# First four heads loaded head by head on two queues, the first two chunks' order rewritten, constants set by VectorE, one share moved by two groups

## The chip, the cores and the metric

The kernel runs on one core of a Trainium2 chip. The core has a matrix engine (TensorE, written PE in the profile, with its weight loads as PEld), VectorE (DVE), ScalarE (ACT), GpSimd (POOL) and SyncE (SP), which here only issues DMAs. The five run side by side, each through its own instruction list in order, and wait for one another on semaphores. The metric is the device time of one execution in microseconds (us); lower is better. Three executions of the kernel before took 309.56, 308.94 and 307.16 us (median 308.94). A further execution, the one with the profile, took 308.46 us; its span from the first to the last instruction is 306.7 us, so 1.76 us lie around the span.

## The reference, cut to what matters

```python
# q, k, v: (4, 8, 768, 64) float32; proj: (64, 6); x has 4 x 768 rows of 512
q_bits = einsum('bhsd,dk->bhsk', q, proj) > 0        # 6 sign bits: the bucket; k likewise
mask   = q_bucket[:, :, :, None] == k_bucket[:, :, None, :]
scores = where(mask, scale * q @ k.T, -1e9)
attn   = softmax(scores)
x      = (attn @ v) as (batch, seq, heads * 64)
xn     = (x - mean) / sqrt(var + 1e-6) * g_ln
out    = x + relu(xn @ w_ch1) @ w_ch2                # 512 -> 2048 -> 512
```

Attention looks only at keys whose 6 hash bits equal those of the query. An MLP with a residual follows.

## The kernel before, in words

The work is 12 chunks: 4 batches x 3 chunks of 256 queries. A chunk has 12 units (`att_units`), four pairs of heads by three groups of key blocks. Unit u has four steps: S (scores: four matmuls into one `sc` tile, L452), X (one exp over 128x1024 on ScalarE, L462), V (eight matmuls of the exps with the values into `av`, L487; the first unit of a pair adds one matmul with the key epsk, L476, in batch 0), and, at the third unit of a pair, D (the division on VectorE, L505 to L514). Then the chunk's MLP runs (row statistics L533, centring L539, up products L596 with a relu each on DVE or ACT, down products L637 and the residual L642), spread as filler between the units of the next chunk.

The mask comes without a comparison: 6 bits as +-1/2 are put beside the 64 rows of each query and key in `slots`, so one matmul over 70 rows gives score and match together, and the exp makes a mismatch vanish.

Batch 0 has to be prepared before any attention can start, head by head. T(h) (L204, four transposes on PE) turns three pairs of key blocks and the first pair of query blocks of head h; E (L223 DVE, L221 ACT) copies the result out of PSUM, scaled; C casts its halves into `slots` (L248 DVE, L240 ACT, L242 POOL); H (L258, PE) hashes two heads at once; B (L268, DVE) compares with zero and writes the even bits; O (L240 ACT, L242 POOL) copies the odd bits. The same words with an L in front (LT, LE, LC, LH, LB, LO) do the remaining query blocks of two heads together, which chunks 1 and 2 need. vc casts values (L357, POOL), su and sd sum them (L381 PE, L388 DVE). T uses the PSUM bank `av1`, or `av0` where the word ends with an engine's letter, and the bank is free again when E and the C that read it are done. K is a run of idle matmuls that wake PE (L783), J puts the projection in place (L797, DVE), w starts weight and batch-1 loads from POOL's queue, n, ns, xt, xe, U, R are the first chunk's MLP, na, bl and op the preparation of batch 1 by DMA transposes.

For chunks 0 and 1 the order of all these steps is written out by hand in the string `opening`, played by `first_two`; each engine receives its own instructions in that order. From chunk 2 on, `interleave` places fillers between the units by cost, and two small tables add single steps: `singly` (squares on ACT) and `shares`. A share (L371, L372) is for batches 1 to 3: one matmul broadcasts the sum of values over partitions into the `av` bank that the running pair doesn't use, and DVE copies it to `vsum`; D adds it. The next pair's V takes that same bank.

Loads: `load_half` (L124 to L147) fetches q and k of four heads. For the first four heads of batch 0 it cuts the load at 0, 1, 2, 4: heads 0 and 1 singly (q from SP's queue, k from ACT's), heads 2 and 3 together, both q and k from SP's queue. Behind them on SP's queue come the values of heads 0 to 3, q and k of heads 4 and 5, q and k of heads 6 and 7, the second half of the values, and eight small loads of proj.

At the end every engine reads a flag (L939) and branches over a general path (L940) that isn't taken with these data. Two hints for that branch are given to DVE and ACT, before the last down products.

Of the kernel before, what the change touches and what calls it, by code (L numbers as in the profile page):

```python
# [18 lines left out]
LBIT = BIT * BIT  # L19

Q_SCALE = 2.0**-12
# [3 lines left out]
EPS_KEY = 2.0**-100  # L25
# [5 lines left out]
def kernel(  # L31
# [11 lines left out]
    nc = tc.nc  # L43
    P = 128

    B, H, S, D = q.shape
    n_bits = proj.shape[1]
# [9 lines left out]
    D1 = D + 1  # L57
    scale = 1.0 / math.sqrt(D)
# [5 lines left out]
    with tc.manual_schedule():  # L64
# [8 lines left out]
    identf = consts.tile([P, P], F32)  # L73
    make_identity(nc, identf)
    expb = consts.tile([P, 2], F32)
    nc.gpsimd.memset(expb[:, 0:1], -scale * n_bits * 0.25 / Q_SCALE)
    nc.gpsimd.memset(expb[:, 1:2], -scale * n_bits * LBIT)
    ident = consts.tile([P, P], BF16)
    make_identity(nc, ident)
    epsk = consts.tile([P, P], BF16)  # L80
    nc.gpsimd.memset(epsk, EPS_KEY)
    mhalf = consts.tile([P, TT], F32)
    nc.gpsimd.memset(mhalf, -0.5)
    sq = consts.tile([P, 2, 4 * B], F32)

    NG, DG = P // 32, D // 32
# [14 lines left out]
    vaug = [  # L101
        consts.tile([P, H, NC, D1], BF16, name=f"vaug{i}", tag=f"vaug{i}") for i in range(2)
    ]
# [2 lines left out]
    vsplit = consts.tile([P, H, D1], BF16)  # L106
    vsum = [consts.tile([P, H, D], F32, name=f"vsum{i}", tag=f"vsum{i}") for i in range(2)]
    for i in range(2):
        nc.gpsimd.memset(vaug[i][:, :, :, D:D1], 1.0)

    main = ExitStack()
    nat = main.enter_context(tc.tile_pool(name="nat", bufs=4))
# [16 lines left out]
    def load_half(b, half):  # L129

        h0 = half * H // 2
        t = {}
        for nm in "qk":
            t[nm] = nat.tile([P, H // 2, NC, D], F32, tag=f"{nm}nat", name=f"{nm}nat")

        cuts = [[0, 1, 2, 4] if half == 0 else [0, 2, 4], [0, 4], [0, 2, 4], [0, 2, 4]][b]
        for lo, hi in zip(cuts, cuts[1:]):
            for nm, src in (("q", q), ("k", k)):
                eng = nc.gpsimd if b == 1 else nc.scalar if nm == "k" and hi - lo == 1 else nc.sync
                eng.dma_start(  # L140
                    out=t[nm][:, lo:hi],
                    in_=src[b, h0 + lo : h0 + hi].rearrange("h (p c) d -> p h c d", p=P),
                )
        if b == 0 and half == 0:
            nc.scalar.activation(wake2[:, 0:1], wake2[:, 1:2], AF.Exp)
            t["v"] = load_values(b, half)
        return t  # L147

    def load_values(b, half):
        h0 = half * H // 2  # L150
        eng = nc.gpsimd if (b, half) == (1, 0) else nc.sync
        if (b, half) == (0, 1):

            t = work.tile([P, NH * CT // 2], F32, tag="h", bufs=1, name="vnat1")[
                :, 0 : H // 2 * NC * D
            ].rearrange("p (h c d) -> p h c d", h=H // 2, c=NC)
        else:
            t = nat.tile([P, H // 2, NC, D], F32, tag="vnat", bufs=1, name="vnat")
        eng.dma_start(
            out=t, in_=v[b, h0 : h0 + H // 2].rearrange("h (p c) d -> p h c d", p=P)  # L160
        )
        return t
# [3 lines left out]
    class Prep:  # L166
# [7 lines left out]
        def load(self, half):  # L174
            self.tiles.setdefault(half, {}).update(load_half(self.b, half))
# [573 lines left out]
    def chunk_tile():  # L749
# [4 lines left out]
    mlp = {0: mlp_steps(*chunks[0], xs[0])}  # L754

    opening = """
        K26 T0 E0d T1d C0.1g E1a J0 C0.0p C1.1g H0 T2 C1.0g E2a T3d B0 O0g B1 E3d C2.0a S0 C3.0p X0
        O1g LT0 C2.1g vc0 C3.1g S1 H1 X1 S2 LE0d T5d T4 B2 X2 O2g su0 E4a B3 w0 E5d S3 C4.0a sd0 T6d
        H2 E6d B4 C5.0a V0 C4.1a T7 O3g S4 V1 C5.1g E7d X3 O4a V2 X4 S5 vc1 H3 C7.1p B5 D2 V3d S6 X5
        C6.1g B6 X6 O5g V4 LT1d B7 S7 X7 C6.0g V5 C7.0g LE1d su1 O7g D5 S8 LH0 sd1 O6g X8 S9 LC1.0p  # L760
        V6d S10 X9 LB0 V7 LT2d LC0.0g w1 V8 LE2d LO0g LC0.1g D8 S11 LT3d LB1 X10 S12 LE3d X11 V9d w2
        X12 V10 V11 S13 V12 LC3.0g D11 S14 X13 n0 LO1g LC1.1g n1 LH1 ns1 S15 LC2.1g ns0 V13 X14 S16
        V14 LB2 xt0 LB3 X15 LC2.0g V15 xe0d LO2g S17 X16 S18 bl3 V16 bl0 LO3g U0 D14 X17 U1 V17 X18
        R0a S19 LC3.1g R1d V18 X19 bl2 U2 S20 R2d U3 w3 X20 S21 U4 D17 R3a X21 V19 S22 R4a na0 U5
        bl1 R5a X22 na1 S23 U6 V20 U7 V21 D20 R6d S24 R7d V22 X23 V23 X24 nr0 op0 D23
    """

    def first_two():
# [91 lines left out]
    singly = {  # L860
        2: "Q00", 3: "Q01", 4: "Q10", 5: "Q11", 6: "Q20", 7: "Q21", 8: "Q30", 9: "Q31",
    }
    shares = {2: {8: "E10"}, 3: {5: "E11"}, 5: {1: "E20", 10: "E21"}, 7: {1: "E30"}, 8: {1: "E31"}}
    parts_left = {}

    def prepare(op):
# [53 lines left out]
    with tc.manual_schedule():  # L920
        held["up"](NH // 2 - 1)
        norm[1]()
        held["relu"](NH // 2 - 1, nc.scalar)
        for _, f in tail:
            f()
        for n2 in range(NH // 2):
            parts["up"](n2, True)
            parts["relu"](n2, nc.scalar if n2 % 2 else nc.vector)
        for _, f in downs[: 4 * (TT - 1)]:
            f()  # L930
        tc.mark_branch_hint_location(
            "general", "LikelyTaken", [nc.vector.engine, nc.scalar.engine]
        )
        for lo in range(0, d_model, d_model // 2):
            parts["columns"](TT - 1, lo, lo + d_model // 2)
    main.close()


    ok = nc.values_load(flag[0:1, 0:1], min_val=0, max_val=1)  # L939
    with tc.If(ok < 1, label="general"):  # L940
        general_path(
            tc, q, k, v, proj1, gbc, n_bits, w1_sb, w2_sb, identf, ident, out,
        )
# [192 lines left out]
```

## Time and profile before

| what | value |
|---|---|
| three executions | 309.56, 308.94, 307.16 us |
| profiled execution, its span | 308.46 us, 306.7 us |
| PE busy | 296.0 us, 97% of the span |
| DVE, ACT, POOL busy | 181.6, 213.6, 92.1 us |
| chunks 0 and 1 with their preparation end on PE | about 47.5 us after the start |

The page of the profile has the busy time of each engine, the chain of work that ended last and the costliest groups. A row of the timeline reads: start in us, duration in us, engine, line, operation, what it writes <- what it reads with shapes, count; a bracket gives how long the engine was idle before and what released it. Consecutive equal instructions are merged into one row, whose duration goes from the first start to the last end. PE's matmuls overlap, so a group's neighbour may start before the row ends.

### The profile page before, as it was taken

To read this page: it belongs to the slowest core of one execution; us is meant where nothing else is said; L and a number is where in the kernel's file an instruction comes from. 1 tells how busy PE (TensorE), PEld (TensorE's weight loads), DVE (VectorE), ACT (ScalarE), POOL (GpSimd) and SP (SyncE) were. 2 spreads that over 40 slices of the span, in tenths; PEclk is the share of its full clock that TensorE was granted. 3 is DMA by queue.
4 is the path that set the end of the run, shared out by engine and by line. 5 is a ranking of instruction groups with operands and counts; after the bars stand their busy time and mean duration, and the time that the engine had idled before them with its cause. 6 is when DMAs were issued, how large, how long until landed. Compare 5 with 4: busy or idle time off the path is not lost.

```text
span 306.7 us, 7751 instructions
## 1 busy us (share of the span) xinstructions
PE 296.0 (97%) x3207; PEld 223.8 (73%) x3234; DVE 181.6 (59%) x395; ACT 213.6 (70%) x266; POOL 92.1 (30%) x125
## 2 busy tenths in 40 slices
PE   7899999999999999999999999999999999999993
PEld 5567796688688678678688678679688688687662
DVE  2788947665486577645865874734734645555421
ACT  2788887676887787688698688778698578574020
POOL 5878751813430154160650740100100100100100
PEclk9999999999999999999999999999999999999999
DMA  7999999468597747985396573230200200200302
GB/s 231 377 187 286 230 305 199 111 107 208 108 316 125 176 150 142 174 273 145 96 232 141 151 146 85 49 82 0 71 36 0 71 36 0 71 36 0 106 0 78
DMA packets 64969, 40.93 MB, mean 133 GB/s; under 512 B 47152, under 2 KB 59952, under 8 KB 64928
## 3 DMA queue, kind: packets, MB, share of 16 engines
q1 hardware_dynamic: 60224, 31.59, 42.2%
q0 software_dynamic: 4128, 8.13, 11.5%
q10 hardware_dynamic: 576, 0.66, 0.6%
q8 instruction: 27, 0.44, 0.6%
q14 instruction: 14, 0.11, 0.1%
HBM read 27.98 MB, written 6.88 MB: 114 GB/s over the span
## 4 chain that ended last, share of the span: by engine, by line
PE 91%; DMA 3%; DVE 3%; issue 1%; SPq 1%; DVEq 0%
PE hp L596 27%; PE o L637 24%; PE sc L452 20%; PE av L487 11%; PE hash L327 3%; DMA knat<-in_k_dram 2%; PE tpose L204 2%; PE hash L258 1%; PE o L619 1%; DMA qnat<-in_q_dram 1%; DVE xn L539 1%; PE av L476 0%; PE sums L381 0%; DVE stats L533 0%; SPq L140 0%
## 5 line engine op out<-in xcount | busy, mean ns | idle before, releaser
L462 ACT ACTIVATE ex<-sc,expb 128x1024 bf16<-128x1024 f32 x144 | 159.3, 1113 | 54.9 <-PE sc L452 52.7
L596 PE MATMUL hp<-xnT,w_sb 128*128 128x256 bf16 x768 | 98.3, 272 | 0.0
L637 PE MATMUL o<-w_sb,hbuf 128*128 128x512 bf16 x341 | 89.8, 379 | 1.2
L452 PE MATMUL sc<-slots 70*128 70x256 bf16 x576 | 86.7, 272 | 0.2
L596 PEld LDWEIGHTS <-w_sb 128*128 128x128 bf16 x768 | 71.9, 98 | 8.7 <-DMA xnT<-xn 0.5
L487 PEld LDWEIGHTS <-ex 128*128 128x128 bf16 x1152 | 54.0, 98 | 15.3 <-issue 1.8
L452 PEld LDWEIGHTS <-slots 70*128 70x128 bf16 x576 | 51.8, 97 | 15.6 <-issue 1.0
L487 PE MATMUL av<-vaug,ex 128*128 128x65 bf16 x1152 | 58.8, 194 | 0.6 <-DVE vsum L372 0.4
L606 DVE TENSOR_SCALAR hbuf<-hp 128x512 bf16<-128x512 f32 x48 | 32.9, 688 | 40.1 <-PE hp L596 40.0
L637 PEld LDWEIGHTS <-hbuf 128*128 128x128 bf16 x368 | 33.5, 97 | 25.4
L550 POOL TENSOR_SCALAR rs<-mv 128x2 f32<-128x2 f32 x12 | 8.1, 672 | 145.8 <-DVE mv L534 145.6
L608 ACT ACTIVATE hbuf<-hp 128x512 bf16<-128x512 f32 x48 | 28.5, 595 | 19.2 <-PE hp L596 19.2
L642 DVE SCALAR_TENSOR_TENSOR x<-o,rs,x 128x512 f32<-128x512 f32 x23 | 17.0, 740 | 18.4 <-PE o L637 18.4
L514 DVE TENSOR_TENSOR x<-av,rc 128x256 f32<-128x256 f32 x48 | 20.4, 424 | 1.6
L507 DVE TENSOR_SCALAR rc<-av 128x4 f32<-128x4 f32 x36 | 5.7, 158 | 25.1 <-PE av L487 25.1
L539 DVE SCALAR_TENSOR_TENSOR xn<-x,mv,gbc 128x512 bf16<-128x512 f32 x24 | 18.4, 772 | 0.7
L533 DVE BATCH_NORM_STATS2 stats<-x 128x6 f32<-128x512 f32 x24 | 16.5, 689 | 0.4
L357 POOL CAST vaug<-vnat 128x1536 bf16<-128x1536 f32 x8 | 11.8, 1471 | 16.4 <-DMA vnat<-in_v_dram 16.3
L508 DVE TENSOR_TENSOR av<-av,vsum 128x256 f32<-128x256 f32 x36 | 15.6, 433 | 1.2
L288 POOL CAST nat<-qnat 128x1536 bf16<-128x1536 f32 x6 | 8.8, 1466 | 18.5 <-issue 8.4
L293 DVE STREAM_TRANSPOSE bt<-qnat 128x768 f32<-128x768 f32 x12 | 11.3, 958 | 3.8 <-DMA qnat<-in_q_dram 3.8
L184 ACT ACTIVATE knat<-knat 128x768 f32<-128x768 f32 x16 | 13.4, 836 | 0.0
(85 smaller groups left out, 209.0 us busy)
## 6 DMA issues: line engine op xcount, KB each, us to landing
out_dram<-x SPq DMA_DIRECT2D x23, 256.0 KB
vnat<-in_v_dram SPq DMA_DIRECT2D x7, 768.0 KB
qnat<-in_q_dram SPq DMA_DIRECT2D x11, 384.0 KB
knat<-in_k_dram SPq DMA_DIRECT2D x11, 384.0 KB
w_sb<-in_moe_w_ch_dram POOLq DMA_DIRECT2D x4, 1024.0 KB, 12.9
slots<-slots SPq DMA_DIRECT2D x6, 384.0 KB
qnat<-in_q_dram POOLq DMA_DIRECT2D x2, 768.0 KB, 8.5
knat<-in_k_dram POOLq DMA_DIRECT2D x2, 768.0 KB, 10.0
```

Of the source, the lines that this page charges most:

```text
L452: nc.tensor.matmul(sc[:, i, :], key_block(h, kj), query_blocks(h),)
L462: nc.scalar.activation(ex, sc, AF.Exp, bias=expb[:, 1:2] if b else expb[:, 0:1], scale=scale if b else scale / Q_SCALE,)
L487: nc.tensor.matmul(av[:, h - ha, qi, :], state[g][:, i, qi * P : (qi + 1) * P], va[:, h, kj, :], start=(b > 0 and (g, i, qi) == (0, 0, 0)) ...
L508: nc.vector.tensor_tensor(num, num, vs[:, ha : ha + 2, :].unsqueeze(2).to_broadcast([P, 2, TT, D]), op=AOP.add,)
L514: nc.vector.tensor_tensor(xv, num, rc.unsqueeze(3).to_broadcast([P, 2, TT, D]), op=AOP.mult)
L533: nc.vector.bn_stats(stats, x[:, i, :])
L539: nc.vector.scalar_tensor_tensor(xn[:, :, i, :], x[:, i, :].rearrange("p (o d) -> p o d", d=P), mv[:, i, 0:1], gbc.rearrange("p (o d) -> p ...
L596: nc.tensor.matmul(hp[:, i, :], w1_sb[:, dt, nt * P : (nt + 1) * P], st["xnT"][:, dt, :], start=(dt == 0), stop=(dt == ND - 1),)
L606: nc.vector.tensor_scalar_max(dst, src, 0.0)
L608: nc.scalar.activation(dst, src, AF.Relu)
L637: nc.tensor.matmul(o2, st["h"][:, nt, i * P : (i + 1) * P], w2_sb[:, nt, :], start=(nt == 0), stop=(nt == NH - 1),)
L642: nc.vector.scalar_tensor_tensor(x[:, i, :], o2, st["rs"][:, i : i + 1], x[:, i, :], op0=AOP.mult, op1=AOP.add,)
```

## The change

- For heads 0 to 3 of batch 0, q and k are loaded head by head: q of heads 0, 1, 2, 3 from SP's queue, k of heads 0, 1, 2, 3 from ACT's queue.
- The string `opening` holds the same steps in another order, on partly other engines (the letter at a word's end: a ACT, d DVE, g POOL, p DVE from PSUM), with 34 waking matmuls for 26.
- Six constants (two of the exp's biases, epsk, mhalf, the ones column of both `vaug`) are set by DVE instead of POOL.
- The share E11 (batch 1, heads 4 to 7) stands at unit 7 of chunk 3 instead of unit 5.
- The branch hints and the branch's label are gone.

```diff
-    nc.gpsimd.memset(expb[:, 0:1], -scale * n_bits * 0.25 / Q_SCALE)
-    nc.gpsimd.memset(expb[:, 1:2], -scale * n_bits * LBIT)
+    nc.vector.memset(expb[:, 0:1], -scale * n_bits * 0.25 / Q_SCALE)
+    nc.vector.memset(expb[:, 1:2], -scale * n_bits * LBIT)
...
-    nc.gpsimd.memset(epsk, EPS_KEY)
+    nc.vector.memset(epsk, EPS_KEY)
...
-    nc.gpsimd.memset(mhalf, -0.5)
+    nc.vector.memset(mhalf, -0.5)
...
-        nc.gpsimd.memset(vaug[i][:, :, :, D:D1], 1.0)
+        nc.vector.memset(vaug[i][:, :, :, D:D1], 1.0)
...
-        cuts = [[0, 1, 2, 4] if half == 0 else [0, 2, 4], [0, 4], [0, 2, 4], [0, 2, 4]][b]
+        cuts = [[0, 1, 2, 3, 4] if half == 0 else [0, 2, 4], [0, 4], [0, 2, 4], [0, 2, 4]][b]
...
-        K26 T0 E0d T1d C0.1g E1a J0 C0.0p C1.1g H0 T2 C1.0g E2a T3d B0 O0g B1 E3d C2.0a S0 C3.0p X0
-        O1g LT0 C2.1g vc0 C3.1g S1 H1 X1 S2 LE0d T5d T4 B2 X2 O2g su0 E4a B3 w0 E5d S3 C4.0a sd0 T6d
-        H2 E6d B4 C5.0a V0 C4.1a T7 O3g S4 V1 C5.1g E7d X3 O4a V2 X4 S5 vc1 H3 C7.1p B5 D2 V3d S6 X5
-        C6.1g B6 X6 O5g V4 LT1d B7 S7 X7 C6.0g V5 C7.0g LE1d su1 O7g D5 S8 LH0 sd1 O6g X8 S9 LC1.0p
-        V6d S10 X9 LB0 V7 LT2d LC0.0g w1 V8 LE2d LO0g LC0.1g D8 S11 LT3d LB1 X10 S12 LE3d X11 V9d w2
-        X12 V10 V11 S13 V12 LC3.0g D11 S14 X13 n0 LO1g LC1.1g n1 LH1 ns1 S15 LC2.1g ns0 V13 X14 S16
-        V14 LB2 xt0 LB3 X15 LC2.0g V15 xe0d LO2g S17 X16 S18 bl3 V16 bl0 LO3g U0 D14 X17 U1 V17 X18
-        R0a S19 LC3.1g R1d V18 X19 bl2 U2 S20 R2d U3 w3 X20 S21 U4 D17 R3a X21 V19 S22 R4a na0 U5
-        bl1 R5a X22 na1 S23 U6 V20 U7 V21 D20 R6d S24 R7d V22 X23 V23 X24 nr0 op0 D23
+        K34 J0 T0 E0a C0.1g T1d E1a H0 C1.0g C1.1g T2d B0 B1 C0.0g E2a T3 O0g LT1d E3a S0 C2.0g
+        C2.1g H1 O1a C3.0p C3.1p X0 LE1a LC1.0p LT0 B2 S1 LE0a vc0 S2 B3 T4d T5 su0 E4d X1 E5d O3a
+        O2g LC0.0g X2 S3 sd0 w0 T7d H2 E7d V0d C5.1a T6d X3 C4.1g V1 S4 C5.0g V2 B4 E6d C4.0g X4 O4g
+        vc1 C6.0p S5 C6.1p B5 H3 S6 B7 V3 X5 V4 X6 C7.1g O5g su1 S7 O7g V5 X7 S8 X8 B6 O6g sd1 LH0
+        D2 S9 V6d D5 C7.0g V7 LB0 w1 LO0g S10 X9 LT2d X10 LE2d V8 S11 D8 LC0.1g w2 LT3d S12 LB1 V9d
+        LE3d X11 X12 V10 V11 S13 LC3.1g D11 LC1.1g n0 ns0 S14 X13 X14 n1 LO1g LC2.1g LC2.0g LH1 ns1
+        V12d LB2 S15 S16 V13 LB3 V14 LO2g xt0 X15 V15d X16 xe0d na1 D14 bl0 S17 X17 S18 U0 R0a
+        LC3.0g U1 bl3 na0 V16 V17 R1d U2 S19 R2d X18 U3 S20 LO3a V18d X19 V19 X20 R3d bl2 U4 R4d S21
+        V20 X21 S22 X22 U5 U6 D20 bl1 S23 R6a R5d U7 X23 D17 w3 V21d S24 R7d V22 V23 op0 D23 X24 nr0
...
-    shares = {2: {8: "E10"}, 3: {5: "E11"}, 5: {1: "E20", 10: "E21"}, 7: {1: "E30"}, 8: {1: "E31"}}
+    shares = {2: {8: "E10"}, 3: {7: "E11"}, 5: {1: "E20", 10: "E21"}, 7: {1: "E30"}, 8: {1: "E31"}}
...
-        tc.mark_branch_hint_location(
-            "general", "LikelyTaken", [nc.vector.engine, nc.scalar.engine]
-        )
...
-    with tc.If(ok < 1, label="general"):
+    with tc.If(ok < 1):
```

## The prediction

> **What bounds the kernel now.** I read the page's busy times first, then its chain, then the timeline of the first 48 us, last the waits near the end.
>
> ```profile
> span 306.7 us, 7751 instructions
> ...
> PE 296.0 (97%) x3207; PEld 223.8 (73%) x3234; DVE 181.6 (59%) x395; ACT 213.6 (70%) x266; POOL 92.1 (30%) x125
> ...
> PE 91%; DMA 3%; DVE 3%; issue 1%; SPq 1%; DVEq 0%
> ...
> 2.11 6.63 DMA knat<-in_k_dram
> ```
>
> PE is busy for 97% of the span and carries 91% of the chain. So a change that leaves PE's matmuls alone (this one adds eight waking ones) can win only where PE waits. The chain names one such place: a load of k issued at 2.11 us and landed at 2.11 + 6.63 = 8.74. The timeline of the opening shows it from PE's side.
>
> ```profile
> 1.13 2.95 PE L783 MATMUL wakep<-wake 128*128 128x128 bf16 x26 [1.13 <-DVE wake L71]
> 4.25 0.87 PE L204 MATMUL tpose<-identf,knat 128*128 128x128 f32 x3 [0.17 <-DMA knat<-in_k_dram]
> 5.38 0.69 DVE L223 TENSOR_SCALAR qkT<-tpose 128x512 f32<-128x512 f32 x1 [4.22 <-PE tpose L204]
> 5.88 0.60 ACT L221 ACTIVATE qkT<-tpose 128x512 f32<-128x512 f32 x1 [2.73 <-PE tpose L204]
> 6.32 1.29 PE L258 MATMUL hash<-qkT,proj 128*64 128x512 f32 x4 [0.47 <-DVE proj L797]
> 8.48 1.25 POOL L242 COPY slots<-slots 6x512 bf16<-6x512 bf16 x2 [0.42 <-DVE slots L268]
> 8.87 0.52 PE L204 MATMUL tpose<-identf,knat 128*128 128x128 f32 x3 [1.26 <-DMA knat<-in_k_dram]
> 9.33 0.49 PE L204 MATMUL tpose<-identf,knat 128*128 128x128 f32 x3
> 9.77 0.60 PE L452 MATMUL sc<-slots 70*128 70x256 bf16 x4
> 13.96 0.85 PE L381 MATMUL sums<-vaug,wake 128*128 128x260 bf16 x6
> 14.65 0.60 PE L452 MATMUL sc<-slots 70*128 70x256 bf16 x4
> 15.17 0.52 PE L204 MATMUL tpose<-identf,knat 128*128 128x128 f32 x3
> 15.73 1.08 PE L258 MATMUL hash<-spare,proj 128*64 128x512 f32 x4
> 17.17 1.47 POOL L357 CAST vaug<-vnat 128x1536 bf16<-128x1536 f32 x1 [0.60 <-DMA vnat<-in_v_dram]
> 46.98 0.66 PE L487 MATMUL av<-vaug,ex 128*128 128x65 bf16 x16
> ```
>
> PE waits 1.26 us for heads 2 and 3; before that it waits for E and J around H0, and after 15 us nearly nothing. From one start to the next I read PE's prices: a T 0.45 us (8.87 to 9.33), an S 0.44 (a quarter of it is one 128x256 matmul, 0.11 behind the one before; T's four go at the same pace, 9.33 to 9.77), a hash H 1.0 (a little under its row's 1.08), su 0.69 (13.96 to 14.65). The last V of the opening ends at 47.6.
>
> **The constants.** POOL loses six memsets and DVE gains them.
>
> ```profile
> 3.13 0.54 POOL L109 MEMSET vaug<- 128x48 bf16 x2
> 0.90 0.17 DVE L69 MEMSET wake<- 128x128 bf16 x1
> ```
>
> On DVE they cost between nothing and, by the nearest rows, 4 x 0.17 + 0.54 = 1.2 us. DVE was idle for 4.22 us before 5.38 (row above), and POOL's next work waits for E0 in any case. Hidden on both sides: 0; without that cover, the 1.2 us.
>
> **Loads.** ACT issues four DMAs for two; it was idle for 2.73 us before its first copy (the row at 5.88), which covers two issues: 0. SP has as many entries ahead of the values as before. What can move is landing.
>
> ```profile
> 3.00:4.00 1.00, 1.00 (x11) 0.81 (x8) 0.00 (x0) 0.15 (x1) 0.67 (x5) 1.00 1.08 400
> 5.00:6.00 1.00, 0.85 (x6) 0.51 (x4) 0.62 (x1) 0.12 (x1) 0.00 (x0) 1.00 0.90 217
> 6.00:7.00 1.00, 0.68 (x3) 0.38 (x4) 0.92 (x3) 0.48 (x1) 0.79 (x2) 1.00 0.95 316
> 8.00:9.00 1.00, 0.13 (x1) 0.16 (x2) 0.97 (x2) 0.00 (x0) 0.58 (x2) 1.00 1.06 395
> ```
>
> The last column is GB/s. While both queues had work (3 to 4 us) 400 GB/s came in; with SP's alone 217 and 316 in 5 to 7 us, then 395. A head's q and k are 0.39 MB, 1 us at 400. Heads 2 and 3 then land near 5.7 and 6.8; at the slow rate, near 6.3 and 7.8. Heads 6 and 7 landed about 15.1: the values behind them, 0.79 MB, released POOL at 17.17, and 0.79 MB at 395 GB/s take 2.0 us. All bytes ahead of them are the same, so they land at 15.1 again, or up to (400 - 217 + 400 - 316) x 1 us = 0.27 MB, 0.7 us, earlier if two queues fill the slow stretch.
>
> The Trainium skill (DMA: Bandwidth & Descriptors, section "Issuing engines are not separate DMA queues") says that DMAs issued by several engines run on the same 16 DMA engines and interleave, so that a second queue saves only issue time. By that rule the landing of heads 6 and 7 stays and the opening wins 0.2 us instead of the 0.45 taken below; the trace agrees in 8 to 9 us, where one queue alone had 395 GB/s, and speaks against it in 5 to 7 us.
>
> **The new order, worked forward with these prices.** 34 waking matmuls at 2.95 / 26 = 0.11 us hold PE until 4.85, so T0 starts 0.6 later than at 4.25. E0 runs on ACT from 5.75, E1 behind it on the same engine until 6.95 (0.60 each; before, DVE and ACT shared them), so H0 starts at 7.0 instead of 6.32 and PE is free at 8.0. There heads 2 and 3 have landed: T2 at 8.0, T3 at 8.45. LT1 wants the bank of T2, which E2 on ACT frees at 9.25; it runs from 9.3. POOL's four casts and O0, 0.63 each (half of the row at 8.48), end at 9.6, so S0 starts at 9.75 (before: 9.77). Then S0, H1, LT0, S1, S2, T4, T5, su0, S3 take 0.44 + 1.0 + 0.45 + 0.88 + 0.90 + 0.69 + 0.44 = 4.8 us: PE is at T7 at 14.5 and waits for heads 6 and 7 until 15.1. Before, PE started its T6 at 15.17. From the same landing the new order has one LT (0.45) less to do and starts about 0.05 earlier. So the 1.26 us saved at heads 2 and 3 goes mostly to the later start and to a new wait at heads 6 and 7.
>
> After that both lists hold the same steps. The first chunk's statistics gate xt in both, since four DVE operations follow the last division:
>
> ```profile
> 33.73 0.62 PE L575 MATMUL xnTp<-ident,xn 128*128 128x128 bf16 x8 [0.15 <-DVE xn L539]
> ```
>
> In the new order two compares stand on DVE between them and xe with fewer scores to cover it, which I put at 0.3 us of PE. ACT's copies change from side to side and lie beside PE. On POOL's queue w0 and w3 keep about their places, w1 and w2 move up by a cast or two, and the casts for op come ahead of w3, whose loads the work in chunk 2 wants many units later: 0. Opening: -0.45 - 0.05 + 0.3 = -0.2 with the old landing, -0.9 with the landing 0.7 earlier; I take -0.45, nearer the old landing; ends -0.9 and +0.8 (heads 6 and 7 a us late).
>
> **The share.** Around it the timeline reads:
>
> ```profile
> 84.80 0.98 DVE L293 STREAM_TRANSPOSE bt<-qnat 128x768 f32<-128x768 f32 x1 [3.77 <-DMA qnat<-in_q_dram]
> 86.33 0.41 DVE L372 COPY vsum<-share 128x256 f32<-128x256 f32 x1
> 86.80 0.41 PE L487 MATMUL av<-vaug,ex 128*128 128x65 bf16 x8 [0.43 <-DVE vsum L372]
> 87.73 0.68 DVE L606 TENSOR_SCALAR hbuf<-hp 128x512 bf16<-128x512 f32 x1
> 88.46 1.03 PE L596 MATMUL hp<-xnT,w_sb 128*128 128x256 bf16 x8
> ```
>
> DVE hung on a transpose whose load was late, the share's copy queued behind it, and the next pair's V, which takes the share's bank, waited 0.43 us for the copy. At unit 7 the share uses the other bank, which the next pair wants only at unit 9. The copy leaves DVE before the division and the relu of 87.73 that the matmul at 88.46 follows, so the gain isn't returned there; at its new place, 0.41 us more of DVE stand ahead of a relu and of the division at unit 8. Between -0.43 (the wait) and +0.41 (the copy's length); I take -0.4, by the row of the wait.
>
> **The hints.** How the end looks now, first the instructions of the branch line, then, in a fence of its own, SP's longest wait there:
>
> ```profile
> L940 POOLq COMPARE_BRANCH  x1: 53/53/53, 284.4 to 284.4; - x1
> L940 POOLq EVENT_SEMAPHORE  x1: 17/17/17, 285.0 to 285.0; - x1
> L940 PEldq COMPARE_BRANCH  x1: 3882/3882/3882, 300.5 to 300.5; - x1
> L940 DVEq COMPARE_BRANCH  x1: 84/84/84, 302.4 to 302.4; - x1
> L940 ACTq COMPARE_BRANCH  x1: 68/68/68, 303.2 to 303.2; - x1
> L940 ACTq EVENT_SEMAPHORE  x1: 17/17/17, 303.7 to 303.7; - x1
> L940 DVEq EVENT_SEMAPHORE  x1: 21/21/21, 305.6 to 305.6; - x1
> ```
>
> ```profile
> SPq L1131 <- DVEq L940: 2.2, 1, 2.2
> ```
>
> DVE, hinted, still took 3.2 us from its branch to its next instruction, and SP's last long wait was for it. ACT, hinted, took 0.5; POOL, not hinted, 0.6; PE, not hinted, 3.9. So the hint goes with neither. If ACT without it took PE's 3.9, it would arrive at 307.1, 1.5 after DVE now: +1.5. If DVE took ACT's 0.5, PE would be last at 304.4: -1.2. I take 0, between POOL's and DVE's rows. The Trainium skill (Runtime: NRT & Kernel Launch, "Instruction fetch mechanics") says that a taken branch stalls if its target isn't in the window of fetched pages; that fits ACT, whose skipped path is short, and PE, whose is long.
>
> **Sum.** -0.45 - 0.4 + 0 = -0.85 us. The profiled execution took 308.46 (306.7 and 1.76 around the span), the median of the other three is 308.94; from the middle of these, 308.7, this gives 307.85, in round figures 307.9 us.
>
> **Rivals.**
> - Slower by the branch: ACT's target falls out of what is fetched, ACT becomes last. It decides once ACT needs over 2.4 us (303.2 to 305.6). Full price +1.5: 309.4, slower than before. For it: PE's row; against: POOL's. Chance 0.12.
> - Heads 6 and 7 land late: ACT's queue takes half the engines' time until about 6.5 us, and the values wait on SP for the first landing. Each us past 15.1 costs one; at 16.1 the opening is +0.8 and the whole 308.7 + 0.8 - 0.4 = 309.1. Against it: the bytes ahead are the same. Chance 0.13.
> - The slow stretch of 5 to 7 us fills up: opening -0.9, whole 308.7 - 0.9 - 0.4 = 307.4. For it: 400 GB/s in 3 to 4 us; against it: one queue had 395 in 8 to 9. Chance 0.15. With DVE's branch short as well, 306.2; chance 0.05.
> - Little happens: the queues share what one of them had anyway (395 GB/s in 8 to 9 us), nothing lands earlier, and the share's copy stalls a relu at its new place: opening -0.2, share 0, whole 308.5. Chance 0.12. (This is also what the Trainium skill's page named above would expect of the loads.)
> - My forecast, 307.9 +- 0.6: 0.43.
>
> **How the numbers follow.** Range: from the lowest case (306.2) to the branch rival (309.4), and 0.2 and 0.5 us wider, since the three runs before lie 2.4 us apart: 306.0 to 309.9. About 1% is what a measurement of this kernel can tell from no change: 3.1 us. Faster than that needs every gain at once and more: 0.04. Slower needs the branch, the late landing and a stall that I don't see: 0.06. Within: 0.90.
>
> **What would show it.** Right: T0 near 4.85, H0 near 7.0, no wait of a transpose for knat at 8 to 9 but one near 14.5 to 15.1; the last V of the opening ending near 47.1 instead of 47.6; no wait of V for vsum in chunk 3; DVE again last at the end. Wrong: the opening's end later than 47.6, a relu or hp wait of 0.4 us near 89, ACT 3 us behind its branch.

## The result, and the profile after

The changed kernel takes 310.26 us (median of 21 runs, 308.11 to 312.38); the kernel before took 308.04 us in the same comparison (21 runs, 307.10 to 309.56). The ratio is 1.0063, 95% interval 1.0042 to 1.0085: slower by 0.6%. The interval keeps this clear of zero, though it lies inside the 1% that the forecast took for no change. The forecast was 307.9 us, 306.0 to 309.9: wrong in sign, and the time lies above the range. The profiled execution of the changed kernel took 308.52 us (span 306.8), near the fast end of its runs, so its trace shows less of the loss than most executions have.

The page of the changed kernel, busy times and the chain:

```profile
span 306.8 us, 7794 instructions
...
PE 298.9 (97%) x3242; PEld 225.1 (73%) x3242; DVE 182.2 (59%) x401; ACT 213.8 (70%) x266; POOL 91.1 (30%) x119
...
PE 91%; DVE 3%; DMA 3%; ACT 1%; issue 0%; ACTq 0%
```

Nothing stands out here: PE is as full as before. The opening, PE's timeline after the change:

```profile
4.73 0.85 PE L204 MATMUL tpose<-identf,knat 128*128 128x128 f32 x3
...
6.70 1.34 PE L258 MATMUL hash<-qkT,proj 128*64 128x512 f32 x4 [0.42 <-DVE proj L797]
8.16 0.52 PE L204 MATMUL tpose<-identf,knat 128*128 128x128 f32 x3
...
9.97 0.60 PE L452 MATMUL sc<-slots 70*128 70x256 bf16 x4
...
15.35 0.33 PE L204 MATMUL tpose<-identf,knat 128*128 128x128 f32 x1
...
46.93 0.66 PE L487 MATMUL av<-vaug,ex 128*128 128x65 bf16 x16
```

T0, H0 and T2 come within 0.3 us of where the forecast put them (4.85, 7.0, 8.0), the wait of 1.26 us at T2 is gone, and none took its place at T7. Yet the last V of the opening ends at 46.93 + 0.66 = 47.59, where the kernel before had 46.98 + 0.66 = 47.64. The opening is a draw; the loss lies behind it. SP's timeline, the steps that prepare batch 1, first before, then after the change (a row's duration is that of the issuing instruction, not the time until the data have landed):

```profile
41.62 9.17 SPq L310 DMA_TRANSPOSE slots<-nat  x1
54.74 0.73 SPq L318 DMA_DIRECT2D slots<-slots  x1
...
72.44 0.88 SPq L340 DMA_DIRECT2D bits_d<-bits  x1
76.85 3.04 SPq L346 DMA_DIRECT2D slots<-bits_d  x4
...
81.39 0.52 SPq L140 DMA_DIRECT2D qnat<-in_q_dram  x1
```

```profile
38.76 15.99 SPq L310 DMA_TRANSPOSE slots<-nat  x1
56.84 0.73 SPq L318 DMA_DIRECT2D slots<-slots  x1
...
71.65 2.66 SPq L340 DMA_DIRECT2D bits_d<-bits  x1
78.01 3.04 SPq L346 DMA_DIRECT2D slots<-bits_d  x4
...
82.56 0.52 SPq L140 DMA_DIRECT2D qnat<-in_q_dram  x1
```

The DMA transpose `op` begins to be issued 2.9 us earlier, and its issuing instruction ends 4.0 us later: 16 us for 9. The step behind it waits for it to land and comes 2.1 us late. The lateness isn't handed down evenly: the second bit copy (L340) starts 0.8 us earlier than before, but takes 2.66 us to issue for 0.88 and ends 1.0 us later, and the copies behind it (L346) and the load of chunk 3's q come 1.2 us late. VectorE and PE in chunk 3 turn that into time (after the change; a bracket is the idle time before the row and what ended it):

```profile
85.88 0.98 DVE L293 STREAM_TRANSPOSE bt<-qnat 128x768 f32<-128x768 f32 x1 [4.91 <-DMA qnat<-in_q_dram]
86.79 0.71 DVE L642 SCALAR_TENSOR_TENSOR x<-o,rs,x 128x512 f32<-128x512 f32 x1
```

```profile
87.55 1.03 PE L596 MATMUL hp<-xnT,w_sb 128*128 128x256 bf16 x8 [0.96 <-DVE x L642]
89.22 1.03 PE L596 MATMUL hp<-xnT,w_sb 128*128 128x256 bf16 x8 [0.19 <-DVE hbuf L606]
```

VectorE hangs 4.91 us on the late q (3.77 before). The chain of work that ended last goes through this load in both kernels, first before, then after (start and time to landing):

```profile
81.39 3.39 DMA qnat<-in_q_dram
```

```profile
82.56 3.31 DMA qnat<-in_q_dram
```

The wait of V for vsum, which the moved share was to remove, is gone; but the residual x stands behind the same transpose, it frees the bank that hp needs, and PE waits 0.96 us for that. The hp group of 89.22 started at 88.46 before. So the lead of some 0.05 us that PE had at 47 us, and still has at 83.6 us (an o group starts at 83.61 us for 83.67), has become a lag of 0.76 us. It is 0.86 us once the share's matmul has also run (90.88 for 90.02), and stays: VectorE's last addition starts at 302.64 us for 301.76. That the span is nevertheless as long as the one before (306.8 and 306.7) is due to its end, where VectorE takes 0.6 us from its branch to its next instruction, for 3.2:

```profile
L937 DVEq COMPARE_BRANCH  x1: 72/72/72, 303.3 to 303.3; - x1
L937 DVEq EVENT_SEMAPHORE  x1: 21/21/21, 303.9 to 303.9; - x1
```

What lies on POOL's queue at `op`, before and after:

```profile
36.41 0.77 POOL L140 DMA_DIRECT2D qnat<-in_q_dram  x1
...
38.72 1.46 POOL L288 CAST nat<-qnat 128x1536 bf16<-128x1536 f32 x1
40.13 1.47 POOL L288 CAST nat<-knat 128x1536 bf16<-128x1536 f32 x1
```

```profile
35.31 1.46 POOL L288 CAST nat<-knat 128x1536 bf16<-128x1536 f32 x1 [0.48 <-DMA knat<-in_k_dram]
...
37.28 1.46 POOL L288 CAST nat<-qnat 128x1536 bf16<-128x1536 f32 x1
38.69 0.77 POOL L140 DMA_DIRECT2D qnat<-in_q_dram  x1
```

The casts of `op` changed places with the three loads of w3 (2.3 MB): now the transpose and w3 are issued at the same moment, 38.76 and 38.69. The first weight loads, w0, also come later, at 15.21 us for 13.74. Both were candidates for the cause.

### The profile page after: what moved, and what is told of

It is laid out like the page before. It is cut to its first block, busy times and chain, and to the rows that moved or that the text cites. A ratio compares the mean times of both kernels' runs of the same rounds, so it can differ in the third digit from the quotient of the medians.

```text
span 306.8 us, 7794 instructions
## 1 busy us (share of the span) xinstructions
PE 298.9 (97%) x3242; PEld 225.1 (73%) x3242; DVE 182.2 (59%) x401; ACT 213.8 (70%) x266; POOL 91.1 (30%) x119
## 4 chain that ended last, share of the span: by engine, by line
PE 91%; DVE 3%; DMA 3%; ACT 1%; issue 0%; ACTq 0%
PE hp L596 27%; PE o L637 25%; PE sc L452 19%; PE av L487 11%; PE hash L327 3%; DMA knat<-in_k_dram 2%; PE tpose L204 2%; PE hash L258 1%; PE o L619 1%; DMA qnat<-in_q_dram 1%; DVE xn L539 1%; DVE slots L268 0%; PE sums L381 0%; DVE stats L533 0%; ACTq L140 0%
## 5 line engine op out<-in xcount | busy, mean ns | idle before, releaser
L637 PE MATMUL o<-w_sb,hbuf 128*128 128x512 bf16 x368 | 92.9, 379 | 0.0
L452 PEld LDWEIGHTS <-slots 70*128 70x128 bf16 x576 | 52.0, 97 | 15.5 <-issue 1.3
L606 DVE TENSOR_SCALAR hbuf<-hp 128x512 bf16<-128x512 f32 x50 | 34.3, 686 | 42.0 <-PE hp L596 41.9
L487 PE MATMUL av<-vaug,ex 128*128 128x65 bf16 x1152 | 58.1, 194 | 0.0
L608 ACT ACTIVATE hbuf<-hp 128x512 bf16<-128x512 f32 x46 | 27.3, 594 | 20.2 <-PE hp L596 20.2
```

Of the source, the lines that this page charges most:

```text
L452: nc.tensor.matmul(sc[:, i, :], key_block(h, kj), query_blocks(h),)
L487: nc.tensor.matmul(av[:, h - ha, qi, :], state[g][:, i, qi * P : (qi + 1) * P], va[:, h, kj, :], start=(b > 0 and (g, i, qi) == (0, 0, 0)) ...
L606: nc.vector.tensor_scalar_max(dst, src, 0.0)
L608: nc.scalar.activation(dst, src, AF.Relu)
L637: nc.tensor.matmul(o2, st["h"][:, nt, i * P : (i + 1) * P], w2_sb[:, nt, :], start=(nt == 0), stop=(nt == NH - 1),)
```

## The experiments

Each ratio is to the kernel before on the same chip. First the change in parts.

**Everything but the new order.** The changed kernel with the string `opening` of before.

> The changed kernel with the opening string of the kernel before; loads, constants, share and missing hints as changed. Queue theory (the rewritten order issues the first weight load on POOL 1.5 us later, 15.21 for 13.74, and batch 1's first DMA transpose 2.9 us earlier, 38.76 for 41.62, so that the transpose is slow, SyncE's queue falls behind and the q load that VectorE waits for in chunk 3 is issued at 82.56 for 81.39): the loss is in the order, so this is faster than the kernel before by the end's gain (DVE's branch 0.6 us for 3.2) and the share: about 307.0 us against 308.0. Tail theory (the missing hints make the end longer in most executions): slow as the changed kernel, about 310. Landing theory (k of heads 2 and 3 on ACT's queue makes the landing times vary): also near 310.

Measured: 307.50 us (306.51 to 307.98), ratio 0.9969 [0.9955, 0.9983]. Without the new order the rest of the change is a gain of 0.95 us.

**The new order alone.** The kernel before with the new string.

> The kernel before with the new opening string alone; loads, constants, share and hints as before. Queue theory: all of the loss, and without the shorter end and the moved share: 310 to 311.5 us. Tail theory and landing theory: no loss, within 0.7 us of the kernel before.

Measured: 311.39 us (309.32 to 314.15), ratio 1.0101 [1.0064, 1.0138]. The order alone costs 3.1 us; in its trace `op` took 15.53 us to issue, and V in chunk 3 waited 1.77 us for vsum behind VectorE's hang of 5.11 us.

**The hints alone.**

```diff
-        tc.mark_branch_hint_location(
-            "general", "LikelyTaken", [nc.vector.engine, nc.scalar.engine]
-        )
...
-    with tc.If(ok < 1, label="general"):
+    with tc.If(ok < 1):
```

> The kernel before without the branch hints and the branch's label. Queue theory: the end gets shorter by what DVE loses at its branch now beyond PE, 305.6 - 304.5 = 1.1 us at most: about 307.0 to 307.5 us. Tail theory: 309.5 to 310.5. No effect: 308.0.

Measured: 308.39 us (307.18 to 309.93), ratio 0.9987 [0.9964, 1.0010]: no effect. VectorE's branch without hints, in this kernel:

```profile
L937 DVEq COMPARE_BRANCH  x1: 72/72/72, 303.9 to 303.9; - x1
...
L937 DVEq EVENT_SEMAPHORE  x1: 21/21/21, 307.0 to 307.0; - x1
```

3.1 us from the branch to the next instruction, as with the hint (3.2). So the hints are not why it is 0.6 us in the changed kernel. PE's branch, which never had a hint, changed here instead: 1.3 us to its next instruction (302.0 to 303.3) for 3.9 us before, though as many instructions stand ahead of it (3250). Nothing on record says why.

**The share alone.**

```diff
-    shares = {2: {8: "E10"}, 3: {5: "E11"}, 5: {1: "E20", 10: "E21"}, 7: {1: "E30"}, 8: {1: "E31"}}
+    shares = {2: {8: "E10"}, 3: {7: "E11"}, 5: {1: "E20", 10: "E21"}, 7: {1: "E30"}, 8: {1: "E31"}}
```

> The kernel before with share E11 at unit 7 of chunk 3. My prediction's term: -0.4 us, no wait of V for vsum. Share theory (the copy stalls a relu and the division at its new place): 0 to +0.5 us.

Measured: 307.97 us (307.38 to 311.96), ratio 1.0014 [0.9985, 1.0042]. In its trace PE doesn't wait for the copy to vsum any more, and the time doesn't fall measurably.

So the loss is in the order. The next three change one place of it each.

**w0 earlier.** In the changed kernel:

```diff
-        O2g LC0.0g X2 S3 sd0 w0 T7d H2 E7d V0d C5.1a T6d X3 C4.1g V1 S4 C5.0g V2 B4 E6d C4.0g X4 O4g
+        w0 O2g LC0.0g X2 S3 sd0 T7d H2 E7d V0d C5.1a T6d X3 C4.1g V1 S4 C5.0g V2 B4 E6d C4.0g X4 O4g
```

> The changed kernel with the first weight loads (w0) ahead of O2g in the opening's list: POOL issues them while it would otherwise stand idle for VectorE's compare, at about 12.7 us instead of 15.21 us. Theory (the opening costs time because the loads on POOL's queue begin later, so SP's first DMA transpose lands later and every step behind it on SP's queue with it): the value load of w3 lands 1.5 to 2.5 us earlier than 54.3 us, the step behind the transpose is issued near 55 us instead of 56.84, the q load of chunk 3 near 81 us instead of 82.56, and the median falls by about 2 us against the changed kernel, to 307.5 to 308.5 us. Rival A (it is the early DMA transpose that suffers in the stream of loads): w0 alone changes little, 309.7 to 310.5 us. Rival B (the opening's engine lists themselves cost it): no change either, and PE's lag stands already at 47 us.

Measured: 311.79 us (308.45 to 317.25), ratio 1.0103 [1.0065, 1.0140]. w0 went to 12.18 us as meant, and nothing was won: as the whole cause, the late start fell. On POOL's queue the casts moved up by 1.1 us, and with them `op` to 37.66 and w3 to 37.59. The transpose now took longer still, and the step behind it came at 59.85 us for 56.84 (SP's timeline; then PE's):

```profile
37.66 18.34 SPq L310 DMA_TRANSPOSE slots<-nat  x1
59.85 0.73 SPq L318 DMA_DIRECT2D slots<-slots  x1
```

```profile
87.60 1.05 PE L596 MATMUL hp<-xnT,w_sb 128*128 128x256 bf16 x8 [1.57 <-DMA xnT<-xn]
90.46 1.03 PE L596 MATMUL hp<-xnT,w_sb 128*128 128x256 bf16 x8 [1.13 <-DVE x L642]
```

**w3 earlier.** In the changed kernel, w3 back ahead of the casts:

```diff
-        V12d LB2 S15 S16 V13 LB3 V14 LO2g xt0 X15 V15d X16 xe0d na1 D14 bl0 S17 X17 S18 U0 R0a
+        V12d LB2 S15 S16 V13 LB3 V14 LO2g xt0 X15 V15d X16 xe0d w3 na1 D14 bl0 S17 X17 S18 U0 R0a
...
-        V20 X21 S22 X22 U5 U6 D20 bl1 S23 R6a R5d U7 X23 D17 w3 V21d S24 R7d V22 V23 op0 D23 X24 nr0
+        V20 X21 S22 X22 U5 U6 D20 bl1 S23 R6a R5d U7 X23 D17 V21d S24 R7d V22 V23 op0 D23 X24 nr0
```

> The changed kernel with w3 ahead of na1 on POOL's queue, as the old order had it, so that the last loads are issued near 35.3 us instead of 38.69 and both casts, and with them SP's first DMA transpose, come 2.3 us later (near 41.1 us instead of 38.76); w0 stays at 15.2 us. Theory (late start of the stream of loads): the stream still ends near 54 us, the step behind the transpose is still issued at 56.5 to 57 us, and the median stays at 309.7 to 310.5 us. Rival A (the transpose was issued too early, into the loads, and took 16 us instead of 9): it takes some 10 us again, the step behind it is issued near 55 us, and the median falls to 307.5 to 308.5 us.

Measured: 307.51 us (306.57 to 308.33), ratio 0.9976 [0.9950, 1.0001]. The whole loss is gone, with w0 still late (15.46 us). The step behind the transpose is issued 1.3 us sooner than in the changed kernel. SP's timeline:

```profile
40.80 12.65 SPq L310 DMA_TRANSPOSE slots<-nat  x1
55.55 0.73 SPq L318 DMA_DIRECT2D slots<-slots  x1
```

**The load of chunk 3's q earlier on SP's queue.** In the changed kernel:

```diff
-        2: "n d d H10 d d x N11 J10 d N11 B11 d T11 B11 V10 d B11 W11 d B11 u P11 u H11 u J11 u V11 u u u u",
-        3: "n L20 d d d d W20 d d N20 d N20 B20 d T20 u B20 u u B20 u u B20 P20 u u u",
+        2: "n d d H10 d d x N11 J10 d N11 B11 d T11 B11 V10 d B11 W11 d B11 u P11 u H11 u L20 J11 u V11 u u u u",
+        3: "n d d d d W20 d d N20 d N20 B20 d T20 u B20 u u B20 u u B20 P20 u u u",
```

> The changed kernel with the load of batch 2's first half (L20) moved on SP's queue from chunk 3 to chunk 2, ahead of the four bit copies J11, behind which it stood: it is issued near 74.5 us instead of 82.56, and VectorE's B20 in chunk 3 finds its data. Theory (the whole loss is turned into time at one place, where VectorE stands for 4.9 us behind this load, with x of L642 and hp behind it): PE's lag of 1.1 us that arises between 86 and 89 us is gone, and the median falls by 1.5 to 2.5 us against the changed kernel, to 307.7 to 308.7 us, with less spread than 308.1 to 312.4. Rival A (several places lose it, chunk 3 only some of it): 309.3 to 310 us. Rival B (the four loads, ahead of the bit copies, only hold up what follows on SP's queue): 310.3 us or more.

Measured: 311.38 us (309.30 to 312.93), ratio 1.0117 [1.0085, 1.0149]: no better than the changed kernel, and what the rival expected by which the four loads hold up what follows on SP's queue. VectorE's hang on q is gone, but PE now waits for other steps of the same queue, the bit copies J11 and the transpose of xn:

```profile
83.81 0.61 PE L452 MATMUL sc<-slots 70*128 70x256 bf16 x4 [0.66 <-DMA slots<-bits_d]
...
87.02 1.05 PE L596 MATMUL hp<-xnT,w_sb 128*128 128x256 bf16 x8 [1.49 <-DMA xnT<-xn]
```

The trace fits that rival. The second transpose of `op` was issued 0.5 us earlier here than in the changed kernel (64.62 us for 65.12), but J11, behind the loads, 0.3 us later (78.31 for 78.01). The transpose of xn took 5.35 us from issue to landing; in the changed kernel it was issued at 81.16 us, and PE used it at 84.85 without a wait. So this move is no cure, but it brings a delay of its own, and the run doesn't tell one late load from a late queue. What speaks for the queue is the chain that ended last: it passes through the load of q before, after, and in the slow kernels with the new order alone, with w0 earlier and with the swap below. In the four kernels with the moved share that issue this load no later than before (everything but the new order, w3 earlier, w3 with w2, both moves) it stays on PE all through chunk 3.

**The constants alone.** The kernel before with the six memsets on VectorE, the first hunks of the change:

```diff
-    nc.gpsimd.memset(epsk, EPS_KEY)
+    nc.vector.memset(epsk, EPS_KEY)
...
-        nc.gpsimd.memset(vaug[i][:, :, :, D:D1], 1.0)
+        nc.vector.memset(vaug[i][:, :, :, D:D1], 1.0)
```

> The kernel before with only the six constants set by VectorE. The two kernels with them so far had VectorE's last branch 0.6 us long, those without 3.2 us, hinted or not, and the end 0.8 us nearer to the last addition of L623. Theory (six more instructions on VectorE shift where its code behind the branch lies, and so its tail; the hints do nothing): VectorE's branch takes 0.6 us, from the start of the last L623 to the end 4.1 us instead of 4.9, and the median is 0.5 to 1.0 us below before. Rival (the short branch came with the missing hints together with something else): the branch stays at 3.2 us, and the median within 0.3 us of before.

Measured: 307.16 us (306.12 to 308.05), ratio 0.9977 [0.9961, 0.9994], a gain of 0.7 us, with the hints in place. VectorE's branch in this kernel:

```profile
L940 DVEq COMPARE_BRANCH  x1: 84/84/84, 302.8 to 302.8; - x1
L940 DVEq EVENT_SEMAPHORE  x1: 21/21/21, 303.4 to 303.4; - x1
```

0.6 us for 3.2. Its trace records 451 instructions of VectorE ahead of its branch here, 449 or 450 in all the others with these constants, and 444 or 445 in those without them, where the branch takes 3.1 to 3.3 us, hinted or not. The gain is shown by this run; that it hangs on the count, or on where the code lies, is not.

Then, what it is about w3 and the casts: that the transpose is issued early, or that w3 comes behind it.

**w3 far ahead, the transpose early.** In the changed kernel, w3 right behind w2:

```diff
-        D2 S9 V6d D5 C7.0g V7 LB0 w1 LO0g S10 X9 LT2d X10 LE2d V8 S11 D8 LC0.1g w2 LT3d S12 LB1 V9d
+        D2 S9 V6d D5 C7.0g V7 LB0 w1 LO0g S10 X9 LT2d X10 LE2d V8 S11 D8 LC0.1g w2 w3 LT3d S12 LB1 V9d
...
-        V20 X21 S22 X22 U5 U6 D20 bl1 S23 R6a R5d U7 X23 D17 w3 V21d S24 R7d V22 V23 op0 D23 X24 nr0
+        V20 X21 S22 X22 U5 U6 D20 bl1 S23 R6a R5d U7 X23 D17 V21d S24 R7d V22 V23 op0 D23 X24 nr0
```

> The changed kernel with w3 right behind w2 on POOL's queue (near 28.5 us instead of 38.69), the casts na1 and na0 where they were, so SP's first DMA transpose is issued early again, between 37.5 and 39.5 us. Theory 1 (the transpose was issued too early into the weights of w2, which still stream until about 43 us): it takes 15 us or more, the step behind it is issued at 56.5 us or later, and the median stays at 309.5 to 310.5 us. Theory 2 (what matters is that w3's loads were queued behind the transpose instead of ahead of it, so that both run at the same time for longer): with the loads ahead of it the transpose ends by 53.5 us, the step behind it is issued by 55.6 us, and the median is 307 to 308.3 us, as with w3 ahead of na1.

Measured: 308.63 us (306.94 to 310.16), ratio 1.0015 [0.9992, 1.0038]. w3 was issued at 28.03 us. Neither theory holds alone:

```profile
38.51 14.54 SPq L310 DMA_TRANSPOSE slots<-nat  x1
55.13 0.73 SPq L318 DMA_DIRECT2D slots<-slots  x1
```

The early transpose takes long (the first theory), but the step behind it comes at 55.13 and most of the loss is gone (the second): from +0.63% to +0.15%, where w3 ahead of na1 brought -0.24%.

The length of the issuing instruction is a poor measure of the loss, as the GB/s of the changed kernel show (30 to 60 us, 40 slices of 0.75 us):

```profile
GB/s 408 406 375 381 247 221 209 214 203 210 206 205 218 205 202 206 209 213 347 368 364 371 401 362 208 414 354 151 13 165 83 62 74 290 269 0 0 53 154 154
```

From 33.75 to 43.5 us the engines move about 200 to 220 GB/s; the two loads of w2 (1 MB each, issued at 26.73 us, median landing 16.2 us later) are under way then. The transpose is issued at 38.76 us, in the middle of this. In the kernel before, the stretch ends near 42 us, and the transpose is issued at 41.62. The rate rises near 43 us in the two kernels with w3 moved as well, and there the issuing instruction ends at 53.05 us (w3 with w2) and 53.45 (w3 ahead of na1), though it begins 2.3 us apart, against 54.75 in the changed kernel. So most of the extra 6.8 us in the changed kernel fits an early issue into a stretch that is slow in any case (4.7 us from 38.76 to 43.5); what w3's place changes here is the end, by 1.3 to 1.7 us.

**The old order with this one swap.** The kernel before:

```diff
-        R0a S19 LC3.1g R1d V18 X19 bl2 U2 S20 R2d U3 w3 X20 S21 U4 D17 R3a X21 V19 S22 R4a na0 U5
-        bl1 R5a X22 na1 S23 U6 V20 U7 V21 D20 R6d S24 R7d V22 X23 V23 X24 nr0 op0 D23
+        R0a S19 LC3.1g R1d V18 X19 bl2 U2 S20 R2d U3 X20 S21 U4 D17 R3a X21 V19 S22 R4a na0 U5
+        bl1 R5a X22 na1 w3 S23 U6 V20 U7 V21 D20 R6d S24 R7d V22 X23 V23 X24 nr0 op0 D23
```

> The kernel before with w3 behind na0 and na1 instead of ahead of them, nothing else: the two casts come at some 36.4 us and 37.9 us, SP's first DMA transpose and w3's loads both start near 39.3 us, w0 stays at 13.7 us. Theory (this place of w3 and the casts on POOL's queue is the whole loss of the new order): the transpose takes 15 to 18 us instead of 9.2, the step behind it is issued 2 to 4 us later than 54.7 us, and the median is 2 to 3 us above before, about 310 to 311 us. Rival (with w0 as early as before, its late start being the other half of the loss, there is room enough): within 0.7 us of before.

Measured: 311.77 us (310.03 to 314.35), ratio 1.0114 [1.0066, 1.0162]. One word moved in the old order costs what the whole new order cost (1.0101). SP's timeline, PE's, and what the 16 DMA engines moved in the same 40 slices from 30 to 60 us, here and, last, in the kernel before:

```profile
39.07 16.48 SPq L310 DMA_TRANSPOSE slots<-nat  x1
58.15 0.73 SPq L318 DMA_DIRECT2D slots<-slots  x1
```

```profile
86.28 1.03 PE L596 MATMUL hp<-xnT,w_sb 128*128 128x256 bf16 x8 [1.58 <-DMA xnT<-xn]
89.61 0.41 PE L487 MATMUL av<-vaug,ex 128*128 128x65 bf16 x8 [1.86 <-DVE vsum L372]
```

```profile
GB/s 377 324 244 223 210 206 209 206 208 205 216 227 193 205 210 244 355 300 265 318 218 193 237 231 210 202 223 202 185 181 135 40 41 64 289 238 57 0 0 89
```

```profile
GB/s 375 366 257 216 209 205 210 208 206 202 217 206 225 194 208 257 361 435 381 383 383 357 333 301 283 146 53 310 156 6 188 80 51 0 21 154 153 143 199 329
```

Before, 283 to 435 GB/s come in from the 17th slice on (42 us), and the rate falls off after the 25th (49 us). With the transpose and w3 together it is 181 to 237 from the 21st slice (45 us) until the 30th (52.5 us).

**Both moves.** The changed kernel with w0 ahead of O2g and w3 ahead of na1 (the diffs of the two above).

> The changed kernel with both moves: w0 ahead of O2g and w3 ahead of na1. Theory (the transpose has to come behind w3's loads; the earlier the stream of loads begins, the better): w0 near 12.2 us, w3 near 34 us, the transpose near 39.7 us in 9 to 12.5 us, the step behind it by 55 us, median 306.5 to 307.5 us, no worse than with w3 alone. Rival (the time at which the transpose is issued is what counts, and below about 40 us it is too early): the transpose takes over 14 us, and the median is 309 us or more.

Measured: 306.85 us (306.49 to 307.68), ratio 0.9962 [0.9946, 0.9979]: 1.2 us faster than before, the lowest ratio of all, though the intervals of several others overlap it, and faster than the changed kernel, which is above 308 us in every run. Whether the early w0 adds anything to w3's move (0.9976 [0.9950, 1.0001] by itself) these intervals don't tell; the queue does run earlier:

```profile
40.58 9.79 SPq L310 DMA_TRANSPOSE slots<-nat  x1
53.88 0.73 SPq L318 DMA_DIRECT2D slots<-slots  x1
```

**The loads alone.** The kernel before with heads 0 to 3 cut singly:

```diff
-        cuts = [[0, 1, 2, 4] if half == 0 else [0, 2, 4], [0, 4], [0, 2, 4], [0, 2, 4]][b]
+        cuts = [[0, 1, 2, 3, 4] if half == 0 else [0, 2, 4], [0, 4], [0, 2, 4], [0, 2, 4]][b]
```

> The kernel before with only the loads of heads 0 to 3 cut head by head on the two queues. Theory (they cost and bring nothing that lasts, since PE's place at T7, some 15.1 us, is set by other engines): T2 without the wait of 1.26 us for k, T7 at 15.0 to 15.2 us all the same, median within 0.4 us of before. Rival (where the second pair of heads lands late, the whole kernel is late, and smaller cuts land sooner): 0.5 to 1 us below before, T7 earlier than 15 us.

Measured: 307.72 us (307.18 to 308.71), ratio 0.9975 [0.9947, 1.0003]: between a gain of 1.6 us and nothing. PE starts the transposes of heads 6 and 7 earlier than 15 us and without a wait, against my theory:

```profile
14.48 0.52 PE L204 MATMUL tpose<-identf,knat 128*128 128x128 f32 x3
```

Alone, the five parts come to -0.7 (constants), -0.8 (loads), +0.4 (share), -0.4 (hints) and +3.1 us (order), in sum +1.6; together they measure +1.9 (0.63% of 308.04). The middle three each have an interval that holds zero.

## Why the prediction was wrong, step by step

- **The step that failed** is the sentence on POOL's queue: "On POOL's queue w0 and w3 keep about their places, w1 and w2 move up by a cast or two, and the casts for op come ahead of w3, whose loads the work in chunk 2 wants many units later: 0." It asked who waits for w3's loads, and rightly found nobody near. It didn't ask what the casts release: a DMA transpose on SP's queue, which then starts in the same moment as w3's loads, and behind which eleven rows of SP's timeline stand in order up to the load of chunk 3's q, with VectorE and PE at the end of them. Undone, it takes 0.87 points of the ratio out (1.0063 to 0.9976), 2.7 us; done alone in the old order, it puts 1.14 in, 3.5 us, where the forecast had 0. The Trainium skill (DMA: Bandwidth & Descriptors, "Issuing engines are not separate DMA queues") says that DMAs of all issuing engines interleave on the same 16; the forecast weighed that rule for the first loads and not for this pair, where the GB/s lines of the swap above agree with it.
- **The base**: the forecast counted from 308.7 us, and 21 runs of the kernel before have a median of 308.04. By itself this put the forecast 0.7 us too high, so the number missed by less than the mechanism did: -0.85 us was forecast, +1.9 us (0.63%) measured.
- **How SP's lateness reaches PE** was in the fence on the share: VectorE already hung 3.77 us on a load there. The forecast read it as a reason to move the share, and not as a sign that everything behind SP's queue had no room left.
- **The share**: the wait of 0.43 us went, as forecast, but alone the move brings nothing measurable (1.0014 [0.9985, 1.0042]). In the changed kernel hp is next to wait, 0.96 us for the residual x, which hangs behind the same late transpose. The forecast looked at the relu behind the copy, not at the bank ahead of hp.
- **The opening**: taken at -0.45, measured -0.05 in the trace. The landing wasn't what held it: with the loads alone, PE starts on heads 6 and 7 at 14.48 us without a wait (15.17 before), near the early end of the forecast's range for the landing. But in the new order PE gets to T7 only at 15.35 and finds the data there: from S0 at 9.97 it took 5.4 us for steps that I had priced at 4.8, and S0 itself was 0.2 us late.
- **The hints**: 0, right. VectorE's short branch, which the forecast had in one rival together with the early landing (chance 0.05), did come, but through a part that I had priced at nothing. So VectorE isn't last at the end, as forecast, but PE, at 305.4 us.
- **The constants**: hidden at the start, as forecast (with the constants alone T0 starts at 3.88 us, before at 4.25); but with them VectorE's branch took 0.6 us for 3.2, and the kernel 0.7 us less. That this was possible stood in the forecast (a branch of 3.2 us that the hint doesn't explain); what decides it didn't, and no run shows it. The Trainium skill (Runtime: NRT & Kernel Launch, "Instruction fetch mechanics") says that a taken branch stalls if its target isn't among the fetched pages; that the length goes with the count of instructions ahead of it fits for VectorE. PE's branch, which became short with the hints gone and the same count, shows that the count alone doesn't decide it. No run here shows the pages themselves.
- **The rivals** of the forecast: two didn't come, since ACT's branch took 0.5 us and PE didn't wait at T7. "Little happens" (opening -0.2, share 0, 308.5 us) was nearest in these two terms, which measured -0.05 and nothing; but it too had 0 for POOL's queue, and so it falls short by 1.8 us as well. No rival had the loss in it.

What stays open: in the changed kernel's own profiled execution the GB/s don't fall from 43.5 to 50 us but for one slice, and neither do they with the new order alone; the drop is seen in the old order with the swap and with w0 alone earlier (125 to 224 GB/s from 44 to 53 us). And how much of the 0.87 points is the early issue and how much w3's place can't be told closely: with w3 far ahead but the transpose early, the ratio lies between (1.0015 [0.9992, 1.0038]).

## What to carry to other kernels

When steps change places on an engine's queue, follow what each of them releases on the other queues as well as who waits for its result; a DMA that is issued earlier may land later. A queue behind which an engine already hangs for some us has no room left: price every shift of it, and a step moved forward in it delays those that it passes (here they stopped PE instead). And measure the parts of a mixed change alone: a gain of about 1 us was hidden here under a loss of 3.

## What the runs showed of the hardware

- The instruction that issues a DMA transpose of one half batch took 9.1 to 12.7 us when it began 5 to 6 us behind the loads of w3 (the kernel before and seven runs), 14.5 us when it began 10 us behind them but at 38.5 us, and 15.5 to 18.3 us when it began with them (the changed kernel and four runs). From its start to the step that waits for its landing it was 13.1 us before and 18.1 us after. In the old order with the swap the DMA engines moved 181 to 237 GB/s for 7 us of this, where before they moved 283 to 435.
- Six instructions more on VectorE, hundreds of instructions ahead of a branch, went with 0.6 us from the branch to the next instruction in place of 3.2 us, in every kernel that has them. Without the branch hints VectorE's branch still took 3.1 us.
- Runs spread widely with w0 alone earlier, 308.5 to 317.3 us, and little with both moves, 306.5 to 307.7. Spread isn't peculiar to the late transpose, though: with the share alone it was 307.4 to 312.0.
